# Moving four loads of a linear-attention and feed-forward kernel to later places in the load queue

## The chip, the cores and the metric

The kernel runs on one core of one Trainium2 chip. The metric is the device time of one execution in microseconds (us); lower is better. The core has a matrix engine (TensorE, PE in the profile), a vector engine (VectorE, DVE), a scalar engine (ScalarE, ACT), GpSimd (POOL) and SyncE (SP), which here only issues transfers. Each engine works through its own instructions in order and waits on semaphores for the others. Transfers (DMAs) run beside the engines, on 16 DMA engines that the queues share.

## The reference

The first block is a linear attention with a decaying state (4 batches, 8 heads, 768 tokens, 48 channels a head), the second a feed-forward layer on its output (3072 tokens, 384 channels, 2048 hidden):

```python
for t in range(S):
    cur = np.einsum('bhd,bhe->bhde', u[None] * kt, vt)
    y[:, :, t] = np.einsum('bhd,bhde->bhe', rt, state + cur)
    state = wt[:, :, :, None] * state + np.einsum('bhd,bhe->bhde', kt, vt)
...
h = x @ w_in
sp = np.maximum(h, 0.0) + np.log1p(np.exp(-np.abs(h)))
g = h * erf(sp)
return (g @ w_out)
```

All data is float32 outside, except that the weights arrive as 64-bit floats: the kernel loads them as pairs of 32-bit words.

## The kernel before, in words

**Steps.** The tokens are cut into 12 steps: 6 stretches of 128 tokens by 2 pairs of batches. Step s needs r and k (`in`, 1024 KB, loaded in two halves), w (512 KB) and v (384 KB). The inputs' buffers `in`, `w` and `v` exist twice, so step s + 2 uses the buffers of step s.

**Attention in levels.** Within halves of 64 tokens, the decayed scores are built in six levels. Level l multiplies the right halves of blocks of 2^l tokens with the left ones on TensorE (`level_products`, L552). VectorE then puts the scores into `own` (`take_level`, L562, or L569 on ScalarE for level 6; L773 and L908 for level 1) and scales r and k in place by products of w (`scale`, L321 in step 0, L328 later). Those products of w, `tot_sb`, are made on GpSimd (L350 in steps 0 and 1, L402 from step 2 on). After the levels come the products of scores and v (`from_own`, L584), k turned by TensorE (L817 or L929), the products of the state (`state_part`, L658), which read k and v, and those of r with the state (`through_state`, L610). Step 0 is written out in `attend_first`, steps 1 to 4 in `attend`, the later ones in `attend_late`. In step 0 the second half of the state's products and the sum `S_next` (L852) are held back as `pending` and done in step 1 after level 2's scaling.

**Weights.** There are 16 pairs of weight rows, 0 to 7 of `w_in` and 8 to 15 of `w_out`. Each pair goes through `convert`: stage "l" loads it as two DMAs of 384 KB into a `words` buffer (three of them); "b" (L255, later L257) and "r" (L263) on ScalarE make two parts; "h" (L272) on VectorE shifts one; "o" (L285) on GpSimd adds them. "j" is "h" and "o" together. A load can be held back: `load(i, behind)` first copies one element of another tile into the buffer, on GpSimd (L240) or ScalarE (L238), and the DMA must wait for that copy. `send("brl")` runs the next pair of each named stage.

**Order.** The program order inside each engine is written out by hand (`manual_schedule`), SP's too, so a DMA on SP that waits holds up all that follow on SP. In step 1, each level calls `early` (stage "j" of one pair, before the level is taken) and then `place` (stages "b", "r", mostly "l" of later pairs, then a piece of the feed-forward layer of step 0: L1018, twelve matmuls of `hidden`, and the copy L1027 on ScalarE). The first pieces of `hidden` need xT of step 0: `through_state` copies y (L618), `hop` mixes it (L625) and copies xT (L631); `hop` also issues the loads of pair 3, behind xT, and pair 4. The tile `m` in PSUM exists twice, so a piece waits for the copy L1027 of the piece two before it.

**The loads around the change, in SP's order before:** pair 1 (level 2 of step 0), v[0], w[1], w[2], v[1], pair 2 (behind `own` after level 6), pair 3 and pair 4 (in `hop`), v[2] (`load_third`, after `pending`), pair 5 (`place` of level 2 of step 1), the two halves of in[2], pair 6 (level 3), pair 7 (level 4), pair 8 (level 5), pair 9 and w[3] (level 6).

Of the kernel before, what the change touches and what calls it, by code (L numbers as in the profile page):

```python
# [20 lines left out]
HC = 64  # L21
# [40 lines left out]
def kernel(  # L62
# [14 lines left out]
    nc = tc.nc  # L77
# [99 lines left out]
        nc.scalar.copy(t[:, 0, 0, 0:1], behind)  # L177
        load_halves(t, rkw[1])

    def load_third():  # L180
        t = ins.tile([P, 2, JP, C], FP32, name="in")
        vt = ins.tile([P, NH, D], FP32, name="v")
        loaded[2] = t, vt
        load_v(2)

    def load_v(s):

        vt = loaded[s][1]
        nc.sync.dma_start(out=vt[:], in_=v[s])
# [113 lines left out]
    def rows(e, n=D):  # L303
        return slice(e * EP, e * EP + n)
# [440 lines left out]
    def attend_first(xT):  # L745


        for _ in prepare(0):
            pass
        totals = plan_totals(0)  # L750
        c, _, vt, made, S, S_next, ends = parts_of(0)
        t5 = turns["first"]
        own = att.tile([P, NH, HC], FP32, name="own")
        halves = [range(j * NP, (j + 1) * NP) for j in range(NJ)]
        batch = JP * C // 2 // NJ
        pp = products([P, NE, JP, HC])
        for half in halves:
            level_products(pp, by_pair(made), 1, half)
            stay_warm(2)
        nc.scalar.copy(first[:], mask_sb[:, 0, :])  # L760
        totals(1, part=slice(0, batch))
        for j in range(NJ):
            scale(0, 1, batch=j)
        load_second(t5[:, 1, 0, NP - 1, 1:2])

        def wait_for(t):

            nc.gpsimd.tensor_copy(out=block_sb[:, 0:1], in_=t5[:, 1, 0, NP - 1, t : t + 1])

        wait_for(1)  # L770
        totals(1, part=slice(batch, 2 * batch))
        totals(2, part=slice(0, batch // 2))
        nc.vector.tensor_mul(  # L773
            own[:], pp[:].rearrange("p e n t -> p (e n) t"),
            first[:, None, :].to_broadcast([P, NH, HC]),
        )
        behind = {3: (3,), 4: (4, 5), 5: (6,)}
        for level in range(2, LOG):
            pp = turns.pop("pp", None) or products([P, NE, JP, HC])
            for j, half in enumerate(halves):  # L780
                level_products(pp, first_pair, level, half)
                scale(0, level, batch=j)
            turns["pp"] = products([P, NE, JP, HC])
            keep_busy(turns["pp"], (DM,))
            take_level(own, pp, level)
            wait_for(1 << level - 1)
            if level == 2:
                totals(2, part=slice(batch // 2, batch))
            else:
                totals(*behind[level])  # L790
            if level == 2:
                stages["b"](0, 0)
                stages["b"](0, 1)
                stages["r"](0)
                for _ in prepare(1):
                    pass
                stages["l"](1, own[:, 0, 2:3])
                nc.sync.dma_start(out=vt[:], in_=v[0])
                nc.sync.dma_start(out=ws[1][:], in_=rkw[1][:, 2])
                load_w(2)  # L800
                load_v(1)
        totals = plan_totals(1)
        pp = turns.pop("pp")
        for j, half in enumerate(halves):
            level_products(pp, first_pair, LOG, half)
            scale(0, LOG, batch=j)
        take_level(own, pp, LOG)

        kT = att.tile([P, NH, D], FP32, name="kT", bufs=1)
        kT_by_e = kT[:].rearrange("p (e n) d -> p e n d", e=NE)  # L810
        turned = [products([P, NE, JP, HC])]
        keep_busy(turned[0], (DM,))
        for j, half in enumerate(halves):
            if j:
                turned.append(products([P, NE, JP, HC]))
            for i, n in enumerate(half):
                nc.tensor.transpose(  # L817
                    turned[j][:, 0, 2 * i : 2 * i + 2], first_pair(1, n), ident[:]
                )
        from_own(0, own, 1)  # L820
        for half, ps, copy in zip(halves, turned, (nc.scalar.copy, nc.vector.tensor_copy)):
            copy(
                kT_by_e[:, :, half.start : half.stop],
                ps[:, 0].rearrange("p (n e) d -> p e n d", e=NE)[..., :D],
            )
        stages["l"](2, own[:, 0, HC // 2 : HC // 2 + 1])
        stages["b"](1, 0)
        stages["b"](1, 1)
        fence()
        stages["h"](0)  # L830
        stages["h"](0)
        ps = [[products([P, NE, JP, HC], 1 - e)[:, e] for e in range(NE)]]
        state_part(0, kT, ps, (0,))
        from_own(0, own, 0)
        nc.scalar.copy(middle[rows(1)], ps[0][1][rows(1), :, :D])
        nc.vector.tensor_copy(middle[rows(0)], ps[0][0][rows(0), :, :D])
        stages["r"](1)
        stages["h"](1)
        stages["h"](1)
        wait_for(HC - 1)  # L840
        stages["o"](0)
        nc.gpsimd.tensor_mul(faded[1][:], middle[:], ends[:, :, 1:2].to_broadcast([P, JP, D]))
        totals(1)
        stages["o"](1)
        totals(*range(2, LOG + 1))
        through_state(0, xT)

        def pending():
            part = products([P, NE, JP, HC], turns["next"])[:, 0]
            state_part(0, kT, ps + [[part] * NE], (1,))  # L850
            for e in range(NE):
                nc.vector.tensor_add(S_next[rows(e)], faded[1][rows(e)], part[rows(e), :, :D])  # L852

        turns["pending"] = pending

# [18 lines left out]
    def attend(s, xT, early, place, behind):  # L874
# [11 lines left out]
        for level in range(near_log(s) + 1 if s == DIRECT else 1, LOG + 1):  # L886
            rk = by_pair(made) if level == 1 else RK
            pp = turns.pop("pp", None) or products([P, NE, JP, HC])
            if s == level == 1:
                level_products(pp, rk, level, range(NP))  # L890
                turns.pop("hop")()
                level_products(pp, rk, level, range(NP, JP))
                send("br")
            elif s != 2 or level != 2:
                level_products(pp, rk, level)
            if level == LOG and s == DIRECT:
                spread_blocks(s + 1, pp)
            if s == 1 and level == LOG:
                early(level - 1)
            scale(s, level)  # L900
            if s == 1 and level == 2:
                turns.pop("pending")()
                load_third()
            if s != 1 or level < LOG:
                early(level - 1)
            got = pp[:].rearrange("p e n t -> p (e n) t")
            if level == 1:
                nc.vector.tensor_mul(  # L908
                    own[:], got, first[:, None, :].to_broadcast([P, NH, HC])
                )  # L910
            else:
                take_level(own, pp, level)
            if level > 1:
                next(following, None)
            if s == 2 and level == 1:

                def ahead():
                    turns["pp"] = products([P, NE, JP, HC])
                    level_products(turns["pp"], RK, 2)

                turns["ahead"] = ahead
            place(level - 1)
            if s == 1 and level == 2:
                load_halves(loaded[2][0], rkw[2])

        from_own(s, own, 1)
        ps = products([P, JP, P])
# [346 lines left out]
    with tc.manual_schedule(  # L1274
# [15 lines left out]
        for s in range(n_steps):  # L1290
# [7 lines left out]
            def place(n):  # L1298
# [7 lines left out]
                if s in ALONE:  # L1306
                    if s == 2 and not n:

                        next(hids[0])
                        turns.pop("ahead")()  # L1310
                    convert_at(n)
                    if (s, n) == (1, LOG - 1):
                        load_w(3)
                    if (s, n) == (2, LOG - 2):
                        load_v(3)
                        nc.sync.dma_start(out=block_sb[:], in_=block_mask)
                        nc.sync.dma_start(out=u_row[:], in_=u_rows)
                    if s == 2 and not n:
                        beside(s, next(places))
                        advance(STAGES[s][n])  # L1320
                        return
                    advance(STAGES[s][n])
                else:
                    advance(STAGES[s][n])
                    convert_at(n)
                    if s == DIRECT - 1 and not n:
                        load_rows(DIRECT)
# [125 lines left out]
```

## Time and profile before

| What | us |
|---|---|
| median of 6 runs (588.48 to 590.86) | 589.61 |
| the profiled execution: its time | 590.34 |
| its span, first to last instruction | 588.5 |
| TensorE busy | 579.7 (98%) |
| VectorE busy | 438.6 (75%) |
| ScalarE busy | 361.1 (61%) |
| GpSimd busy | 271.3 (46%) |

The granted TensorE clock is full throughout. "Busy" of TensorE counts matmuls that are pipelined and whose ends are modelled, so 98% does not mean peak rate. In lists of instructions a line gives the start in us, the length in us, engine, line of the kernel, operation, output <- inputs, how many are merged, and in brackets how long the engine had been idle before and what ended that. In the chain of work that ended last, a line gives start, length and what ran; "issue" is time in which the engine waited for nothing that the profile shows. In a table of stretches a line gives the stretch, its length, the busy time of each engine with its number of instructions, the granted clock, the busy share of the DMA engines, and GB/s.

### The profile page before, as it was taken

How to read it: one execution, taken by the hardware profiler on the slowest of the kernel's cores; microseconds unless marked ns; L12 is line 12 of the kernel's file. 1: busy time of each engine (PE TensorE's matmuls, PEld its weight loads, DVE VectorE, ACT ScalarE, POOL GpSimd, SP SyncE). 2: the span in 40 equal slices, each digit the busy share in tenths (PEclk: the TensorE clock that was granted, in tenths of full speed). 3: DMA queues.
4: the chain of work that ended last, by engine and by line, in shares of the span. 5: the costliest groups of instructions: out<-in, count | busy, mean ns of one | idle time of the engine just before them, and what ended most of it. 6: DMA issues, size and time to landing. Idle time of an engine off the chain costs nothing.

```text
span 588.5 us, 16632 instructions
## 1 busy us (share of the span) xinstructions
PE 579.7 (98%) x7256; PEld 498.2 (85%) x7256; DVE 438.6 (75%) x523; ACT 361.1 (61%) x474; POOL 271.3 (46%) x307
## 2 busy tenths in 40 slices
PE   8899999999999999999999999999999999999997
PEld 6688887688668668998998998998998898898997
DVE  6686886999996899799799799799799525023140
ACT  3658877644444698756766766766766754746720
POOL 3556381703398379469369369369369000000000
PEclk9999999999999999999999999999999999999999
DMA  7695662340342414244334334333331300000000
GB/s 242 237 320 195 217 218 70 154 154 12 142 144 74 133 43 166 42 142 153 57 136 158 57 133 153 65 128 114 74 125 37 74 21 14 3 20 15 1 27 28
DMA packets 54081, 63.24 MB, mean 107 GB/s; under 512 B 35160, under 2 KB 40568, under 8 KB 52984
## 3 DMA queue, kind: packets, MB, share of 16 engines
q1 hardware_dynamic: 53624, 61.98, 33.1%
q8 instruction: 57, 0.93, 0.6%
q10 hardware_dynamic: 384, 0.20, 0.1%
q14 instruction: 16, 0.13, 0.1%
HBM read 52.39 MB, written 8.69 MB: 104 GB/s over the span
## 4 chain that ended last, share of the span: by engine, by line
PE 84%; DVE 9%; ACT 2%; issue 2%; DMA 2%; POOL 0%; SPq 0%; DVEq 0%; POOLq 0%; ACTq 0%
PE m L1018 36%; PE m L1126 28%; PE m L1050 6%; PE pp L552 4%; DVE in L328 2%; PE y L584 2%; PE pp L658 2%; PE y L610 2%; PE m L860 1%; DVE sums L453 1%; DMA words<-in_moe_w_in 1%; DVE words L467 1%; DMA rest<-in_w_rows 1%; DVE rk L463 1%; ACT rest L263 1%
## 5 line engine op out<-in xcount | busy, mean ns | idle before, releaser
L1018 PE MATMUL m<-xT,w_in_sb 128*128 128x256 f32 x1152 | 256.7, 381 | 0.5 <-ACT h L1027 0.4
L1018 PEld LDWEIGHTS m<-xT,w_in_sb 128*128 128x128 f32 x1152 | 216.2, 190 | 31.0 <-ACT h L1027 0.8
L1027 ACT COPY h<-m 128x512 f32<-128x512 f32 x96 | 55.6, 580 | 81.8 <-PE m L1018 81.8
L328 DVE TENSOR_TENSOR in<-in,tot_sb 128x1024 f32<-128x1024 f32 (+1 forms) x55 | 79.3, 1443 | 15.0 <-PE pp L552 13.1
L463 POOL TENSOR_TENSOR rk<-words 128x528 f32<-128x528 f32 (+3 forms) x28 | 42.4, 1514 | 91.1 <-DVE sums L453 80.7
L467 POOL TENSOR_TENSOR words<-words,rest 128x528 f32<-128x528 f32 (+10 forms) x77 | 78.2, 1016 | 6.0
L1050 PE MATMUL m<-w_out_sb,h 128*128 128x384 f32 x192 | 64.3, 491 | 0.0
L1050 PEld LDWEIGHTS m<-w_out_sb,h 128*128 128x128 f32 x192 | 35.7, 190 | 23.5
L1126 PE MATMUL m<-mixed,h 128*128 128x192 f32 x288 | 51.1, 331 | 0.0
L974 ACT ACT_TABLE_LOAD x36 | 46.2, 1283 | 2.5 <-issue 1.9
L1126 PE MATMUL m<-w_out_sb,h 128*128 128x192 f32 x272 | 47.5, 329 | 0.0
L1126 PEld LDWEIGHTS m<-mixed,h 128*128 128x128 f32 x288 | 46.6, 190 | 0.9
L978 ACT ACT_TABLE_LOAD x36 | 46.2, 1283 | 1.6 <-DVE room L1109 1.1
L1126 PEld LDWEIGHTS m<-w_out_sb,h 128*128 128x128 f32 x272 | 44.3, 190 | 0.4
L1126 PE MATMUL m<-w_out_sb,room 128*128 128x192 f32 x256 | 44.2, 326 | 0.0
L552 PEld LDWEIGHTS pp<-in 48*64 48x64 f32 (+1 forms) x2368 | 33.4, 126 | 12.1 <-issue 4.0
L1126 PEld LDWEIGHTS m<-w_out_sb,room 128*128 128x128 f32 x256 | 42.0, 190 | 0.0
L983 DVE TENSOR_TENSOR h<-h,y 128x1024 f32<-128x1024 f32 x17 | 20.7, 1216 | 28.3 <-ACT y L978 28.1
L974 ACT ACTIVATE room<-h 128x1024 f32<-128x1024 f32 x36 | 38.1, 1059 | 0.4
L552 PE MATMUL pp<-in 48*64 48x32 f32 (+1 forms) x2368 | 37.1, 212 | 0.6 <-DVE in L328 0.5
L983 DVE TENSOR_TENSOR h<-h,pp 128x1024 f32<-128x1024 f32 x19 | 23.1, 1214 | 19.1 <-ACT pp L978 19.1
L463 POOL TENSOR_TENSOR words<-words 128x336 f32<-128x336 f32 (+6 forms) x49 | 35.2, 718 | 3.8
(144 smaller groups left out, 824.6 us busy)
## 6 DMA issues: line engine op xcount, KB each, us to landing
in<-in_rkw SPq DMA_DIRECT2D x8, 1024.0 KB, 5.0
words<-in_moe_w_in SPq DMA_DIRECT2D x16, 384.0 KB, 5.4
words<-in_moe_w_out SPq DMA_DIRECT2D x16, 384.0 KB, 4.7
words<-in_rk_rows SPq DMA_DIRECT2D x8, 768.0 KB, 5.6
w<-in_rkw SPq DMA_DIRECT2D x11, 512.0 KB, 5.4
v<-in_v SPq DMA_DIRECT2D x12, 384.0 KB, 5.9
out<-o SPq DMA_DIRECT2D x23, 192.0 KB, 2.8
in<-in_rkw SPq DMA_DIRECT2D x7, 512.0 KB, 5.8
```

The source lines that it names most:

```text
L328: nc.vector.tensor_mul(halves, halves, view(tots[level - 1], 0, [[1, n], [2, nb], [0, half]]))
L463: engine.tensor_mul(terms[n], r[:, :, n:], k[:, :, : near - n])
L467: engine.tensor_mul(k[:, :, :m], k[:, :, :m], w[:, :, n : n + m])
L552: nc.tensor.matmul(to, lhsT=rk(1, n)[rows(e), s0 : s0 + m], rhs=right, start=True, stop=True,)
L584: nc.tensor.matmul(y[at(e, p), e, p // 2, j, t], lhsT=vt[t, n * NE + e, :], rhs=own[t, e * JP + n, :], start=swap == 1 and not j and not q ...
L974: nc.scalar.activation(sp_room, chunks[0], AF.Softplus)
L978: nc.scalar.activation(at, sp_room, AF.Erf)
L983: nc.vector.tensor_mul(h, h, at)
L1018: nc.tensor.matmul(ps[:, ff, :], lhsT=w_in_sb[:, g * FG + f + ff, kk * P : (kk + 1) * P], rhs=xT[:, kk, :], start=kk == 0, stop=kk == KT - 1,)
L1027: nc.scalar.copy(h[:, f : f + FT, :], ps[:])
L1050: nc.tensor.matmul(ps[j][:], lhsT=gs[g][:, f, j * C : (j + 1) * C], rhs=w_out_sb[:, g * FG + f, :], start=g + f == 0, stop=g == NG - 1 and ...
L1126: nc.tensor.matmul(to, lhsT=a[:, f], rhs=b[:, f], start=start and f == 0, stop=f == FG - 1, skip_group_check=True,)
```

## The change

Four loads move. In step 0, after level 2, w[2] and v[1] are no longer issued. Pair 2 ("l" of 2) moves from before the fence to after stage "o" of pair 0, behind `middle` (the state after the first half) in place of `own`. `load_third` moves into `pending`, after `S_next`; it now loads v[1] behind an element of `S_next`, by a copy on GpSimd, and no longer v[2]. w[2] is issued after in[2], in level 2 of step 1. v[2] is issued after w[3], in the `place` of level 6 of step 1. Nothing else is added or removed.

```diff
-    def load_third():
+    def load_third(behind):
+
         t = ins.tile([P, 2, JP, C], FP32, name="in")
         vt = ins.tile([P, NH, D], FP32, name="v")
         loaded[2] = t, vt
-        load_v(2)
+        nc.gpsimd.tensor_copy(out=loaded[1][1][:, 0, 0:1], in_=behind)
+        load_v(1)
...
                 nc.sync.dma_start(out=ws[1][:], in_=rkw[1][:, 2])
-                load_w(2)
-                load_v(1)
...
-        stages["l"](2, own[:, 0, HC // 2 : HC // 2 + 1])
         stages["b"](1, 0)
...
         stages["o"](0)
+        stages["l"](2, middle[:, 0, 0:1])
         nc.gpsimd.tensor_mul(faded[1][:], middle[:], ends[:, :, 1:2].to_broadcast([P, JP, D]))
...
                 nc.vector.tensor_add(S_next[rows(e)], faded[1][rows(e)], part[rows(e), :, :D])
+            load_third(S_next[:, 0, 0:1])
...
                 turns.pop("pending")()
-                load_third()
...
                 load_halves(loaded[2][0], rkw[2])
+                load_w(2)
...
                         load_w(3)
+                        load_v(2)
```

## The prediction

> **What bounds the kernel now.** I read the page's header and chain first. TensorE is busy 98% of the span and 84% of the chain that ended last is TensorE, so an edit in the first 50 us counts only by how far it shifts the step that starts TensorE's unbroken run. Then I read the chain in order of time for 20 to 60 us:
>
> ```profile
> 22.06 0.65 PE pp L658 x20
> 22.71 1.58 issue
> 24.30 0.43 PE pp L658 x10
> ...
> 24.81 0.47 ACT middle L835
> ...
> 28.29 0.93 ACT xT L631 x3
> ...
> 29.83 5.46 DMA words<-in_moe_w_in
> ```
>
> Two things stand out: TensorE stops for 1.58 us in the middle of step 0's state products, waiting for nothing that the profile shows, and ScalarE then waits for weight pair 3, whose load is issued behind xT. The stretches, with the DMA engines' busy share and GB/s last, say why:
>
> ```profile
> 16.00:21.00 5.00, 4.76 (x141) 3.15 (x141) 4.53 (x8) 3.60 (x9) 1.85 (x7) 1.00 1.00 377
> 21.00:25.00 4.00, 2.33 (x98) 1.86 (x97) 1.90 (x5) 1.51 (x4) 1.78 (x1) 1.00 0.93 347
> 25.00:30.00 5.00, 4.66 (x124) 3.77 (x114) 2.40 (x4) 3.27 (x8) 4.55 (x4) 1.00 0.06 19
> ...
> 33.00:37.00 4.00, 4.00 (x89) 3.36 (x86) 3.68 (x4) 1.60 (x2) 0.88 (x1) 1.00 1.00 340
> 37.00:42.00 5.00, 4.60 (x102) 3.87 (x95) 4.97 (x6) 3.27 (x6) 2.50 (x2) 1.00 0.99 386
> 42.00:47.00 5.00, 5.00 (x83) 4.22 (x82) 5.00 (x4) 4.39 (x10) 2.91 (x2) 1.00 1.03 400
> ```
>
> DMA is full from 16 to 25, idle from 25 to 30 and full again from 33 to 47. In the first full stretch the trace's packet records have one 16 KB packet on the instruction queue, at 21.86 (0.91 us long). TensorE's 768th instruction record lies at 18.77; after the 256th (10.99), 512th (15.21) and 1024th (24.79) the next such packet starts 0.0 to 0.6 us later, here 3.1 us. So I take the 1.58 us for a fetch of instructions held up behind data; TensorE goes on 1.5 us after that packet's end.
>
> Last, the timeline of ScalarE (L255 converts pair after pair) and VectorE:
>
> ```profile
> 29.34 0.87 ACT L255 ACTIVATE y<-words 128x768 f32<-128x768 f32 x1
> ...
> 35.40 0.87 ACT L255 ACTIVATE y<-words 128x768 f32<-128x768 f32 x1 [4.34 <-DMA words<-in_moe_w_in]
> ...
> 41.40 0.88 ACT L255 ACTIVATE y<-words 128x768 f32<-128x768 f32 x1 [1.73 <-DMA words<-in_moe_w_in]
> ...
> 45.98 0.89 ACT L255 ACTIVATE y<-words 128x768 f32<-128x768 f32 x1 [0.60 <-DMA words<-in_moe_w_in]
> ...
> 49.07 0.94 ACT L255 ACTIVATE y<-words 128x768 f32<-128x768 f32 x1 [0.90 <-DVE w_in_sb L272]
> ```
>
> These are pairs 2, 3, 5, 6 and 7. Three wait for their words. VectorE runs from 30.24 to 49.04 with idle times of 0.52 and 0.31 us only. So from 30 to 50 the limits are DMA and VectorE, with TensorE close behind (idle 0.7 us).
>
> **The change, part by part.** Sizes: a pair is 2 x 384 KB = 0.79 MB, a v 0.39, a w 0.52, in[2] 1.05.
>
> 1. *The stretch freed.* From 15.7 to 25.2 DMA moves pair 1, v[0], w[1], w[2], v[1] and pair 2: 3.4 MB. Without the last three 1.70 MB are left, at 377 GB/s done by 20.2. The fetch then starts by 20.3 and is of use by 20.3 + 0.9 + 1.5 = 22.7, just where TensorE ran dry. Gain on TensorE between 0 (fetch as late as now) and 1.58; I take 1.5. What is late next is ScalarE: its two L255 on pair 1 end at 23.69, then L835 (0.47), L263 (0.94), L618 (0.37), the hop's L625 (1.58) and L631 (0.93) run in a row: xT at 28.1 in place of 29.2. Gain 1.1, not 1.5.
>
> 2. *Pair 2 behind `middle`.* The copy on GpSimd (0.18 us in the row of 20.67) now stands behind stage "o" of pair 0 (L285, ends 25.03). So SP issues pair 2 at about 25.3 and 25.65, not 20.88. What covers it: DMA idle from 25 to 30. Bounds for its landing: 3.8 us from the second issue (pair 0, issued 8.13, its second L255 at 12.03) and 5.4 (the page's median for these loads). On idle engines pair 0 is nearer: 29.5. L255 on pair 2 starts at 29.5, not 29.34: **+0.15**, and all that ScalarE had won is lost at this wait. Queued behind it on ScalarE are L263 and pair 3's L255; on VectorE, L272 of pair 2 (30.24), then L908 and the level scalings. The other end, 5.4, makes it 31.1. The copy also delays L842 by 0.2 us; the step-1 totals behind it have over 2 us in hand.
>
> 3. *VectorE from 30.4.* L272 0.96, L908 1.22; the 0.52 idle before the scaling of level 2 goes, because TensorE is 1.1 earlier with the products that this scaling overwrites; L328 2.11, L852 1.11: S_next at 35.5, not 36.0. Pair 3, issued 1.1 earlier, is there, so the 0.31 before its L272 goes too: **-0.8** on VectorE from here.
>
> 4. *v[1] behind S_next takes v[2]'s place.* SP is in order. Now:
>
> ```profile
> 33.50 0.33 SPq L189 DMA_DIRECT2D v<-in_v  x1
> 34.01 0.81 SPq L147 DMA_DIRECT2D words<-in_moe_w_in  x2
> 34.86 0.92 SPq L147 DMA_DIRECT2D in<-in_rkw  x2
> ```
>
> v[2] waited for L658 (33.46). v[1] waits for S_next (35.5) and a GpSimd copy (0.2; GpSimd is idle 3.52 us there): issued at 35.8. Behind it on SP stand pair 5 (36.3, 2.3 us later than now), in[2] and w[2]. Meanwhile pairs 3 and 4 are over by about 33.5, so DMA idles some 3 us. v[1] itself is not needed before L584 at 51.79.
>
> 5. *w[2] behind in[2].* Before pair 6 lands there must move, from about 36.8 (1 us after the first issue): v[1], pair 5, in[2], w[2] and pair 6: 3.54 MB. At 386 to 400 GB/s that takes 9.0 us, to 45.8; add 1.5, as pair 2 now lands at 26.7 though DMA is full only to 25.2: 47.3. Bounds: 46.0 (at 426 GB/s, among the best slices of the first full stretch, and 0.9 us to landing) and 48.2 (pair 7 shares as it does now: 0.76 MB more moved before pair 6 landed, at 378 GB/s). Pair 6 landed at 45.9, so its L255 starts 1.3 later, at 47.3. Pair 5 lands near 41.8 by the same count; its L272 is due at 43.4, so it costs nothing.
>
> 6. *Behind pair 6 on ScalarE:* L263 and L1027 now end at 48.17 and pair 7's L255 waits 0.90 for VectorE. So 0.9 of the 1.3 fits, and L255 of pair 7 starts at 49.5: **+0.4**. It decides, through L263, L1027 and L569 (51.17, now 51.6), when step 1's L584 on TensorE (52.39) starts. VectorE's 0.8 is lost here. From that L584 the chain is TensorE nearly without a break to 69 us, and then conversions that are issued from it; I carry the shift 1:1 to the end.
>
> 7. *v[2] behind w[3].* Issued at about 49.5 onto engines idle from 53 on (share 0.02 between 53 and 60); its first reader is L584 at 84.40. No cost: 30 us in hand. w[2]'s first reader is L402 on GpSimd (47.04); it may come 0.5 us late and is off the chain. Per-issue times on SP (0.43) lie in SP's waits.
>
> **Sum:** step 1's L584 moves by +0.15 (pair 2), -0.95 (VectorE's two waits and shorter wait behind), then +1.2 (pair 6 in place of VectorE as the last): +0.4. The profiled execution took 590.34 us, its span 588.5; it would become 590.7. The median of the runs shown is 589.61, 0.73 less, so there I predict **590.0**. A measurement of this kernel can tell about 0.2%, 1.2 us, from no change.
>
> [...]
>
> **Rivals.**
> - *The front gain survives:* pair 6 lands by 46.4, as the best slices allow; then VectorE decides, -0.8: 588.8. If pair 2 also lands in 3.2 us (pair 0's first half: issued 7.76, converted at 10.97), VectorE starts 0.6 sooner: -1.4, 588.2. For: the 0.9 of slack before pair 7. Against: 3 us of idle DMA.
> - *SP's queue held by v[1] makes it slower:* pair 2 lands after 5.4 us, S_next comes at 37.0, so pair 5 is issued at 37.8 and pair 6 lands near 48.8 to 49: L255 of pair 6 2.9 late less 0.9: +2.0, 591.6. It decides once pair 6 lands after 48.1 (0.9 slack plus 1.2). For: pair 3 now takes 5.46 on nearly idle engines. Against: pair 4 is issued right behind pair 3, nothing behind pair 2.
> - *The change doesn't do what it says:* the stop stays. Then `middle` is at 25.3, pair 2 is issued at 25.6, and all of points 4 to 6 come 0.7 later: +1.1, 590.7.
>
> **Chances.** Forecast 0.47, front gain 0.16, SP held 0.22, stop stays 0.15. Faster by over 0.2%: 0.11 (most of the first rival's lower half). Slower by over 0.2%: the second rival, half of the third, and a sixth of the forecast: 0.36. Within: 0.53. Range: 588.5 to 591.6, from the first rival to the second, with the bounds of point 5 (46.0 and 48.2, -0.8 and +1.3) inside.
>
> **What would show it.** Right: no stop of over 0.3 us inside L658 near 22.7; xT's copies end near 28.1; pair 2's L255 at 29.5 marked as waiting for DMA; DMA share low around 34 to 36; v[1] issued near 35.8; pair 6's L255 near 47.3 waiting for DMA; step 1's L584 within 0.5 us of 52.4. Wrong: a stop of TensorE elsewhere by another fetch; DMA over 420 GB/s from 37 on; pair 7's L255 waiting for VectorE still, which would mean a gain; a shift at 52 us that does not reach the end.

## The result, and the profile after

| | before | changed |
|---|---|---|
| median, us | 590.26 (47 runs) | 594.54 (21 runs) |
| profiled execution, us (span) | 590.34 (588.5) | 594.39 (592.6) |
| mean granted TensorE clock, profiled execution | 1.0 | 0.994 |

The ratio is 1.0071, 95% interval 1.0059 to 1.0082: 4.2 us slower, well outside the range given (588.5 to 591.6). Two executions below were slow throughout, the profiled one of e2_pair2_only (667.8 us at a granted clock of 0.85) and one of g4_pair2_scalar_unheld (993.1 us at 0.557), and are left out of the ratios, not of the medians.

The chain of the changed kernel, in order of time. Most lines of code are 1 to 2 higher than before: L257 is L255, L265 L263, L274 L272, L330 L328, L554 L552, L586 L584, L660 L658, L1019 L1018, L1028 L1027; L842, L852 and L908 keep their numbers. In the runs below lines lie a few numbers off (L906 in f2 is L908).

```profile
24.96 1.20 POOL words L242
...
26.55 5.10 DMA words<-in_moe_w_in
...
31.67 0.85 ACT y L257
...
33.42 1.23 DVE own L908
...
34.69 1.52 PE pp L660 x32
36.21 5.17 PE m L1019 x12
41.38 1.06 PE pp L554 x64
```

The stop of 1.58 us inside the state's products is gone. In its place the chain runs through GpSimd's one-element copy, pair 2's load, pair 2's L257, VectorE's L908 and the pending state product. The twelve matmuls behind that take 5.17 us; before, such a group took 2.8. TensorE's timeline before, then that of the changed kernel with its stretches (granted clock third from the end), say why:

```profile
31.59 1.14 PE L552 MATMUL pp<-in 48*64 48x32 f32 x64
32.55 0.91 PE L658 MATMUL pp<-v,kT 64*48 64x48 f32 x32
33.39 2.86 PE L1018 MATMUL m<-xT,w_in_sb 128*128 128x256 f32 x12
36.18 1.14 PE L552 MATMUL pp<-in 48*64 48x32 f32 x64
```

```profile
22.03 0.88 PE L660 MATMUL pp<-v,kT 64*48 64x48 f32 x30
...
30.42 1.14 PE L554 MATMUL pp<-in 48*64 48x32 f32 x64
34.69 1.52 PE L660 MATMUL pp<-v,kT 64*48 64x48 f32 x32 [3.13 <-DVE own L908]
36.14 5.24 PE L1019 MATMUL m<-xT,w_in_sb 128*128 128x256 f32 x12
```

```profile
31.60:34.70 3.10, 0.01 (x2) 0.01 (x2) 2.15 (x3) 2.58 (x4) 1.19 (x2) 0.92 0.86 325
34.70:36.20 1.50, 1.50 (x33) 1.41 (x33) 1.50 (x1) 1.24 (x2) 0.77 (x1) 0.50 0.08 25
36.20:38.00 1.80, 1.80 (x6) 1.45 (x5) 1.75 (x4) 0.00 (x0) 0.19 (x1) 0.50 0.00 0
38.00:41.30 3.30, 3.30 (x9) 2.36 (x7) 1.93 (x2) 1.70 (x2) 1.83 (x1) 0.54 0.69 224
41.30:45.00 3.70, 3.70 (x77) 3.22 (x76) 2.43 (x3) 0.89 (x2) 0.19 (x1) 1.00 0.87 319
```

TensorE is 1.2 us ahead of before at 30.42, then idles 3.13 us, and the clock is halved from 34.18 to 41.0 (6.83 us, by the trace's clock record). The next level's products start at 41.31, not 36.18: 5.1 us late. Of that, 2.1 is the late start of the pending product (34.69 for 32.55) and 3.0 the half clock (0.6 on L660, 2.4 on L1019). Slack later gives 1.2 back: step 1's L586 is through at 57.0, not 53.0, and the span is 4.1 longer. ScalarE's conversions of pairs 2, 3 and 6:

```profile
31.67 0.85 ACT L257 ACTIVATE y<-words 128x768 f32<-128x768 f32 x1 [3.40 <-DMA words<-in_moe_w_in]
...
33.78 0.87 ACT L257 ACTIVATE y<-words 128x768 f32<-128x768 f32 x1 [0.45 <-DMA words<-in_moe_w_in]
...
50.58 0.91 ACT L257 ACTIVATE y<-words 128x768 f32<-128x768 f32 x1 [1.92 <-DMA words<-in_moe_w_in]
```

Pair 2 is 2.3 us later than before, pair 3 is 1.6 sooner, pair 6 4.6 later.

### The profile page after: what moved, and what is told of

Its sections match the earlier page's. It is cut to its first block, busy times and chain, and to the rows that moved or that the text cites. A ratio compares the mean times of both kernels' runs of the same rounds, so it can differ in the third digit from the quotient of the medians.

```text
span 592.6 us, 16635 instructions
## 1 busy us (share of the span) xinstructions
PE 582.7 (98%) x7256; PEld 500.3 (84%) x7256; DVE 435.7 (74%) x523; ACT 361.2 (61%) x474; POOL 271.6 (46%) x308
## 4 chain that ended last, share of the span: by engine, by line
PE 85%; DVE 10%; issue 2%; ACT 1%; DMA 1%; POOL 0%; SPq 0%; DVEq 0%; POOLq 0%
PE m L1019 38%; PE m L1127 28%; PE m L1051 6%; PE pp L554 5%; DVE in L330 2%; PE y L586 2%; PE pp L660 2%; PE y L612 2%; PE m L861 1%; DVE words L469 1%; DVE rk L465 1%; DVE sums L455 1%; DMA words<-in_moe_w_in 1%; PE pp L870 1%; DVE h L1008 1%
## 5 line engine op out<-in xcount | busy, mean ns | idle before, releaser
L1019 PE MATMUL m<-xT,w_in_sb 128*128 128x256 f32 x1152 | 259.2, 384 | 0.1
L1019 PEld LDWEIGHTS m<-xT,w_in_sb 128*128 128x128 f32 x1152 | 217.8, 191 | 31.7 <-ACT h L1028 0.6
L1028 ACT COPY h<-m 128x512 f32<-128x512 f32 x96 | 55.5, 580 | 83.4 <-PE m L1019 83.3
L330 DVE TENSOR_TENSOR in<-in,tot_sb 128x1024 f32<-128x1024 f32 (+1 forms) x55 | 75.5, 1372 | 20.0 <-PE pp L554 13.9
L1127 PE MATMUL m<-w_out_sb,h 128*128 128x192 f32 x272 | 47.5, 329 | 0.0
L554 PEld LDWEIGHTS pp<-in 48*64 48x64 f32 (+1 forms) x2368 | 33.4, 126 | 11.9 <-issue 5.0
L404 POOL TENSOR_TENSOR tot_sb<-tot_sb 128x256 f32<-128x256 f32 (+4 forms) x50 | 36.2, 724 | 3.8
L554 PE MATMUL pp<-in 48*64 48x32 f32 (+1 forms) x2368 | 37.3, 212 | 0.4 <-DVE in L330 0.2
```

Of the source, the lines that this page charges most:

```text
L330: nc.vector.tensor_mul(halves, halves, view(tots[level - 1], 0, [[1, n], [2, nb], [0, half]]))
L404: nc.gpsimd.tensor_mul(new, pair[:, :, 0], pair[:, :, 1])
L554: nc.tensor.matmul(to, lhsT=rk(1, n)[rows(e), s0 : s0 + m], rhs=right, start=True, stop=True,)
L1019: nc.tensor.matmul(ps[:, ff, :], lhsT=w_in_sb[:, g * FG + f + ff, kk * P : (kk + 1) * P], rhs=xT[:, kk, :], start=kk == 0, stop=kk == KT - 1,)
L1028: nc.scalar.copy(h[:, f : f + FT, :], ps[:])
L1127: nc.tensor.matmul(to, lhsT=a[:, f], rhs=b[:, f], start=start and f == 0, stop=f == FG - 1, skip_group_check=True,)
```

## Experiments

The theory, **PS**: two causes, taken to hide one another. P is the late pair 2, which stops TensorE before the pending product. S is the SP queue held by v[1], which makes pair 6 late and stops TensorE before its sixth piece. In either stop the clock may be halved, which adds to it. The rivals were that S alone is the cause, and that the places of w[2] or v[2] are.

Medians are us; ratios are to the kernel before, timed in the same series of runs, with 95% intervals. There were four series (e, f, g, h), in which the kernel before had medians of 591.68, 590.52, 590.68 and 591.22, so a difference of 0.1 or 0.2% between ratios of two series says little.

### e1_pair2_back

The changed kernel with pair 2 in its old place.

```diff
+        stages["l"](2, own[:, 0, HC // 2 : HC // 2 + 1])
         stages["b"](1, 0)
...
-        stages["l"](2, middle[:, 0, 0:1])
```

> The changed kernel with pair 2's load back in its old place (behind own, before the fence); v[1], w[2] and v[2] stay late. Theory P (late pair 2): pair 2's L257 on ScalarE starts at about 28.3 us in place of 31.7, TensorE does not stop before the pending state product (3.1 us in the changed kernel), no half clock near 34 to 41; time 1 us under the kernel before to equal with it, that is ratio 0.998 to 1.000 (about 589.5 where before is 590.3). Theory S (the SP queue held by v[1], so pairs 5 and 6 late): these loads are as late as in the changed kernel, so most of the 4.2 us stays; ratio over 1.004. Theory R (prediction's sum without the late pair 2): pair 6 still eats the gain; ratio 1.000 to 1.001.

Measured: 594.12, ratio 1.0037 (1.0015 to 1.0060). P alone is refuted as the whole cause. The wait for L908 is gone, and half of the loss is still there. TensorE and ScalarE in this kernel:

```profile
47.80 0.76 PE L554 MATMUL pp<-in 48*32 48x32 f32 x64
52.29 5.20 PE L1019 MATMUL m<-xT,w_in_sb 128*128 128x256 f32 x12 [3.74 <-ACT h L1028]
```

```profile
42.32 0.90 ACT L257 ACTIVATE y<-words 128x768 f32<-128x768 f32 x1 [3.23 <-DMA words<-in_moe_w_in]
...
50.03 0.84 ACT L257 ACTIVATE y<-words 128x768 f32<-128x768 f32 x1 [3.73 <-DMA words<-in_moe_w_in]
50.81 0.87 ACT L265 ACTIVATE rest<-words 128x768 int32<-128x768 uint32 x1
51.59 0.56 ACT L1028 COPY h<-m 128x512 f32<-128x512 f32 x1
```

v[1] is issued at 36.13 and pair 6 lands near 50. On ScalarE the copy L1028 of the fourth piece stands behind pair 6's L257 and L265; the sixth piece needs the buffer m which that copy frees. So TensorE idles 3.74 us, and again runs at half clock (from 50.3, 6.83 us). In the changed kernel the same late pair 6 (50.58) stopped nobody, because TensorE was already late by more.

### e4_pair2_seen

As e1, but pair 2 behind the fence's output (`seen`, VectorE's small copy from y), ahead of stage "o".

```diff
         fence()
+        stages["l"](2, seen[:, 0:1])
...
-        stages["l"](2, middle[:, 0, 0:1])
```

> The changed kernel with pair 2's load behind the fence's output (seen, ready near 22.1 us) and ahead of stage o of pair 0 on GpSimd, so issued at about 22.4 us. Theory P: pair 2 lands before xT is ready, its L257 starts at about 28.3 us; as without the move: ratio 0.998 to 1.000. Theory S: ratio over 1.004. If being issued later than 20.9 us is in itself harmful, it stands between e1_pair2_back and the changed kernel.

Measured: 594.07, ratio 1.0042 (1.0018 to 1.0066). As e1: issuing pair 2 as late as this is not harmful in itself, and the loss of e1 is still there. Its profiled execution held the full clock and took 590.73, though TensorE stopped 2.58 us before the sixth piece:

```profile
50.35 2.83 PE L1019 MATMUL m<-xT,w_in_sb 128*128 128x256 f32 x12 [2.58 <-ACT h L1028]
```

### e2_pair2_only

The kernel before with pair 2 alone moved behind middle.

> The kernel before with only pair 2's load moved behind middle. Theory P: the stop of TensorE inside the state products stays (w[2] and v[1] are early), pair 2 is issued at 25.5 to 26 and lands at 30 to 31; its L255 is 1 to 1.7 us late, TensorE waits about 1.2 us for L908 before the pending product, which is too short to halve the clock; time +1 to +1.7 us, ratio 1.002 to 1.003. Theory S: nothing on SP is held longer, ratio 0.999 to 1.001.

Measured: 590.93, ratio 1.0003 (0.9974 to 1.0031). Rather a miss for P, which had 1.002 to 1.003 here: alone, without the front gain, the move costs at most about 1.8 us (the upper end of the interval), perhaps nothing. That 1.2 us of idling is too short to halve the clock is not shown: behind a stop of 1.58 us the profile of the kernel before stayed at 1.0, behind one of 1.18 us f4's (below) went to half.

### e3_warm, g1_warm6, g2_unheld_warm6

Matmuls of the identity in the stop before the pending product: 14, then 6, then 6 together with an SP queue that is not held.

```diff
             if s == 1 and level == 2:
+                warm = ps_m.tile([P, NC, P], FP32, name="m")
+                for _ in range(6):
+                    nc.tensor.matmul(
+                        warm[:], lhsT=ident[:],
+                        rhs=ident[:, None, :].to_broadcast([P, NC, P]),
+                        start=True, stop=True,
+                    )
                 turns.pop("pending")()
```

> The changed kernel with 14 matmuls of the identity into a free buffer m between level 2's products and the pending product of step 1, so that TensorE is busy while pair 2 is awaited (3 us of added work in the 3.1 us stop). Theory P with the clock as the second half of the loss: no half clock from 34 to 41; the twelve matmuls after the pending product take 2.9 us and not 5.2. If the clock alone is left over, the time falls by 2 to 3 us under the changed kernel (ratio to before 1.002 to 1.004). If pair 6, landing at 50.5 us, is right behind as the next limit, only 0.6 to 0.8 us come back (ratio 1.0055 to 1.0065). Theory S without the clock: no change, ratio 1.007.

> The changed kernel with 6 matmuls of the identity (2.7 us) in the 3.1 us stop before the pending product; e3_warm had 6.3 us of them, twice what fits. Theory PS: the clock stays full from 30 to 42, the pending product and the twelve matmuls behind it take 0.9 and 2.9 us (1.5 and 5.2 in the changed kernel), 3 us; but then TensorE waits for pair 6, which lands near 50, before its sixth piece (stop of 2 to 3 us), so little comes back: ratio to before 1.004 to 1.007. If the halved clock alone were what the late pair 2 costs: 1.001 to 1.003.

> f2_pair2_late_unheld (pair 2 late, v[1] not held) with the same 6 matmuls. Theory PS: neither the halved clock nor pair 6 is left, only the late start of the pending product, 2.1 us late against before, some of which later slack takes: ratio 1.001 to 1.003, granted clock 1.0 in most runs. If the clock has no part: as f2_pair2_late_unheld, 1.004.

Measured: e3 598.46, ratio 1.0122 (1.0094 to 1.0151); g1 594.91, 1.0065 (1.0040 to 1.0091); g2 592.65, 1.0036 (1.0012 to 1.0060). e3 was badly sized: its matmuls took 6.31 us, twice what fits. It still shows that with TensorE kept busy there the clock stayed full: all its four runs had 1.0, and the twelve matmuls took 2.86, not 5.24. In g1 the extra tile took a buffer of m, so the next piece waited 1.71 for a copy, and the clock was halved there for 3.41 us; it does not tell the two shares apart. In g2 eight of twelve runs held a clock of at least 0.999, median 591.8. Against 589.6 for the kernel before at that clock (table below) this is 2.2 us of waiting without the clock. That is near the 2.1 read above, though later slack took a part of that one. The whole ratio lies just above what was expected and no better than f2's 1.0040 below, which was the expectation for a clock without a part. So what the clock costs is read from the trace and from the sorted runs (g2 at full clock 591.8, f2 592.5 and 594.1); no ratio shows it.

### f1_back_unheld

Pair 2 in its old place (the diff of e1), and SP not held: w[2] and v[1] behind pair 6.

```diff
-        nc.gpsimd.tensor_copy(out=loaded[1][1][:, 0, 0:1], in_=behind)
-        load_v(1)
...
                 load_halves(loaded[2][0], rkw[2])
-                load_w(2)
+            if s == 1 and level == 3:
+                load_w(2)
+                load_v(1)
```

> Pair 2's load back in its old place, and v[1] no longer held behind S_next: w[2] and v[1] are issued behind pair 6, in level 3 of step 1; v[2] late as in the changed kernel. Theory PS (two independent causes, late pair 2 and the SP queue held by v[1], each enough to stop TensorE for 2.5 to 3.7 us, with the clock halved on top in most runs): both are gone, pair 5 is issued by 31 us, pair 6 lands before 43, TensorE has no stop over 1 us from 20 to 56, and what is left is the front gain: 0.8 to 1.5 us under the kernel before, ratio 0.9975 to 0.9990. If something else in the moved loads costs (w[2] or v[2] in the later stretches), ratio over 1.001.

Measured: 589.94, ratio 0.9983 (0.9968 to 0.9998). Both causes taken away, the loss is gone. v[2] is still late here, so its place costs nothing that shows. ScalarE's pair 6 does not wait (pair 7, behind w[2] and v[1], does):

```profile
44.34 0.91 ACT L255 ACTIVATE y<-words 128x768 f32<-128x768 f32 x1
48.50 0.88 ACT L255 ACTIVATE y<-words 128x768 f32<-128x768 f32 x1 [1.94 <-DMA words<-in_moe_w_in]
```

### f2_pair2_late_unheld

The changed kernel with SP not held (the diff shown under f1); pair 2 stays behind middle.

> The changed kernel with only the hold of v[1] undone (w[2] and v[1] behind pair 6, level 3); pair 2 stays late behind middle. Theory PS: pair 2's L257 waits until about 31.7 us, TensorE stops about 3 us before the pending product and then runs at half clock; pair 6 is in time. As pair 6 was hidden behind this in the changed kernel, little comes back: ratio 1.004 to 1.007. If the held queue alone had been the cause: ratio 0.998 to 1.000.

Measured: 593.47, ratio 1.0040 (1.0020 to 1.0059). P stands without S:

```profile
35.51 1.52 PE L658 MATMUL pp<-v,kT 64*48 64x48 f32 x32 [3.66 <-DVE own L906]
36.96 5.18 PE L1019 MATMUL m<-xT,w_in_sb 128*128 128x256 f32 x12
```

This is the lower edge of what was expected, so undoing S gave back more than PS said (0.3 of 0.7%). Each cause alone costs 0.4% (e1, f2), both together 0.7%, neither nothing (f1). By these times the two nearly add up; that one hides the other is seen in the traces only, one execution each: the late pair 6 stops TensorE in e1 and not in the changed kernel. And P costs 0.4% only along with the front gain: without it, e2's interval ends at 0.3%.

### f3_v1_held_only, f4_w2_only

Of the change only v[1] behind S_next (and v[2] late); only w[2] behind in[2].

> Of the change only v[1] behind S_next in v[2]'s place, and v[2] late; w[2] early and pair 2 in its old place as before. Theory PS: pair 5 is issued near 36.5, pair 6 lands 1.3 us (w[2]'s 0.52 MB) sooner than in e1_pair2_back, at 47.5 to 48.6; TensorE stops 1.5 to 2.5 us before step 1's sixth piece; ratio 1.001 to 1.003. If w[2] behind in[2] is what makes pair 6 late, ratio 0.998 to 1.000.

> Of the change only w[2] behind in[2]; v[1], v[2] and pair 2 as before. Theory PS: SP is not held, pair 6 lands about 1.3 us later than before (47.3), 0.9 of which fits; against it a part of the front gain: ratio 0.999 to 1.001. If w[2]'s place is the cause of e1_pair2_back's loss: ratio 1.003 or more.

Measured: f3 591.96, ratio 1.0014 (0.9997 to 1.0032); f4 590.96, 1.0003 (0.9984 to 1.0022). Both near what was expected; neither interval excludes 1. In f3's trace pair 6's L257 starts at 47.61 and TensorE stops 1.68 us. f4's trace has a stop of 1.62 too, with pair 6 at 50.54; that execution was late from the front on, with half the clock from 25.0. The two together (e1) cost more than the sum of the two medians. So S stands for both, v[1]'s hold and w[2] ahead of pair 6, which f1 and f2 undo together; what each of them costs alone is not shown.

### g4_pair2_scalar_unheld

f2, with pair 2's copy behind middle made by ScalarE right after it makes its half of middle.

```diff
+        stages["l"](2, middle[:, 0, 0:1], True)
         stages["r"](1)
...
-        stages["l"](2, middle[:, 0, 0:1])
```

> f2_pair2_late_unheld with pair 2's copy behind middle made by ScalarE ahead of L263 of pair 1, and not by GpSimd behind stage o: issued at about 24.4 us. Theory PS: the place behind middle is not what costs, but the 1.2 us copy on GpSimd and pair 3 close behind: pair 2 lands by 28.5, its L255 starts within 0.5 us of xT, no stop before the pending product; ratio 0.997 to 0.9995. If any load of pair 2 behind middle is too late: ratio over 1.002.

Measured: 590.46, ratio 0.9991 (0.9970 to 1.0011). The same place in the data, but pair 2 issued 1 us sooner (25.1) and 3 us and more ahead of pair 3: its L255 waits 0.15 us only.

```profile
24.93 0.19 ACT L238 COPY words<-middle 128x1 f32<-128x1 f32 x1
...
29.30 0.88 ACT L255 ACTIVATE y<-words 128x768 f32<-128x768 f32 x1 [0.15 <-DMA words<-in_moe_w_in]
```

### g3_pair3_early, h1_v1_behind_7, h2_seen_v1_behind_7

Attempts at a version better than both: f1 with v[1] behind pair 7; in g3 also pair 3 behind middle; in h2 also pair 2 behind seen.

```diff
             if s == 1 and level == 3:
                 load_w(2)
+            if s == 1 and level == 4:
                 load_v(1)
```

> A version meant to be faster: f1_back_unheld with pair 3's load moved from behind xT to behind middle (copy on ScalarE, issued near 24.3 us, onto idle DMA engines), and v[1] behind pair 7 in level 4. Theory PS: pair 3's L255 starts at 29 to 30 and not 33.8, no ScalarE wait for DMA over 1 us until 50; VectorE is the limit: 0.5 to 1.5 us under f1_back_unheld, ratio to before 0.996 to 0.998. If DMA in that stretch holds up the fetch of instructions again: a stop of TensorE between 24 and 32 and ratio over 0.999.

> f1_back_unheld with v[1] behind pair 7 (level 4) and w[2] behind pair 6. Theory PS with the front stop as the trigger of the halved clock in the kernel before: pair 7's wait of 1.9 us at 48.5 goes, step 1's L584 starts 0.3 to 0.6 us sooner; granted clock 1.0 in most runs against about a third of the runs of before; ratio 0.997 to 0.9985. If f1's gain was an accident of its runs: ratio 0.9995 to 1.001 and as many runs under full clock as before.

> As h1_v1_behind_7, but pair 2's load behind the fence's output (seen), issued near 22.4 us onto idle DMA engines, so that the stretch of the state's products is free of all three loads. Theory PS: as h1_v1_behind_7 or 0.2 to 0.5 us less; ratio 0.9965 to 0.9985, no stop of TensorE over 0.3 us in L658. If pair 2 beside the next instruction fetch costs more than it saves: a new stop between 24 and 30, ratio over 0.999.

Measured: g3 591.43, ratio 1.0002 (0.9985 to 1.0019); h1 589.27, 0.9973 (0.9959 to 0.9987); h2 589.76, 0.9977 (0.9962 to 0.9992). g3 missed: pair 3 came 3 us sooner, but TensorE shows stops marked "issue" of 1.4, 0.8 and 0.5 us between 18 and 60, with the DMA engines at a share of 0.87 to 0.99 during them; each time TensorE goes on 1.2 to 1.5 us after the end of a packet on the instruction queue, as in the kernel before (1.5). h1 and h2 are faster than both kernels, h1 by 0.27%. Where their gain comes from is seen when runs are sorted by their mean granted clock (number of runs, median us):

| kernel | 0.999 and over | 0.996 to 0.997 | 0.994 and less |
|---|---|---|---|
| before (112 runs of four series) | 34: 589.6 | 35: 590.5 | 43: 592.2 |
| changed (22, one more than above) | none | 4: 594.2 | 18: 594.5 |
| e1_pair2_back | 1: 591.8 | 7: 594.1 | 2: 595.0 |
| f2_pair2_late_unheld | none | 5: 592.5 | 7: 594.1 |
| f1_back_unheld | 10: 589.8 | 2: 590.7 | none |
| h1_v1_behind_7 | 10: 589.1 | none | 2: 591.2 |
| h2_seen_v1_behind_7 | 11: 589.7 | none | 1: 591.4 |

6.83 us of half clock in the changed kernel's profile go with a mean of 0.994, 3.41 us in g1's with 0.997. The mean is 0.997 or less in 78 of 112 runs of the kernel before, in 3 of 24 of h1 and h2, in 2 of 12 of f1. At full clock h1 is 0.5 us faster than before, f1 and h2 no faster, so most of their gain is that the clock is kept, and at most 0.5 of the 1 us and more won at xT is in their time. In the profile of before, which happened to hold the full clock, this part of the worth of removing its stop could not be seen. At equal clock e1 is no faster than the changed kernel, as far as so few runs tell: what bringing pair 2 back in time alone wins there shows as fewer runs with 0.994 or less (2 of 10, and 18 of 22).

A halving right behind a stop at the front is seen in two profiles only, f4's (half clock from 24.98) and h1's (from 23.15; there the stop lies just before the state's products):

```profile
24.31 0.43 PE L658 MATMUL pp<-v,kT 64*48 64x48 f32 x11 [1.18 <-issue]
```

```profile
22.83 0.86 PE L584 MATMUL y<-own,v 64*48 64x64 f32 x32 [1.91 <-DMA v<-in_v]
```

That the front stop does this in the runs of the kernel before is inferred: the profiles of f1 and h2, both at full clock, have stops there of only 0.5 and 0.2 us, and most runs of these kernels keep the clock (10 and 11 of 12).

## Why the prediction was wrong, point by point

In short: the sum's +0.15 for pair 2 became +2.3, the path from pair 2 to TensorE was not in it, and a halved clock had no term. The -0.95 for VectorE turned into a loss with pair 2, and pair 6, 4.6 us late and not 1.3, was not what TensorE waited for in this profile.

1. *The stretch freed: right in this profile.* The instruction packet starts at 20.25 (20.3 forecast), 1.5 us behind TensorE's 768th instruction record at 18.75 and not 3.1 as before; the stop goes, and xT's copies end at 28.04 (28.1). That the late packet makes the stop fits the profiles: with it 1.5 us behind TensorE does not stop, with 2.0 (f1) 0.5 us, with 2.3 (g3) 0.8, with 2.8 (f4) 1.2, with 3.1 (before) 1.6, with 3.7 (h1, where the profile names v[0]) 1.9. But the gain is not sure: f2, g1, g2 and e3 have the same front as the changed kernel, and there the packet starts 1.75 to 2.4 us behind and TensorE stops for 0 to 0.8 us.

2. *Pair 2 at 29.5: wrong by 2.2 us, the first step that failed.* Two sizes were off. The copy on GpSimd took 1.19 us, not 0.18:

```profile
23.20 1.83 POOL L287 TENSOR_TENSOR w_in_sb<-w_in_sb,rest 128x768 int32<-128x768 int32 x1 [2.37 <-ACT m L257]
24.96 1.19 POOL L242 COPY words<-middle 128x1 f32<-128x1 f32 x1
```

```profile
24.36 1.75 DVE L330 TENSOR_TENSOR in<-in,w 128x1024 f32<-128x1024 f32 x1
```

These are GpSimd and VectorE of the changed kernel. The copy ends 0.04 us after L330, and likewise 0.05 after it in f2 (26.44 and 26.39) and g2 (26.12 and 26.07). The front gain itself had moved L330 (26.16 before) onto the copy. So the copy took longer beside L330; what couples the two is not shown, nor do the starts show which came first (in g2 the copy's record starts at 24.51, L328's at 24.86). And the load took 5.1 us from its second issue, not 3.8: pair 3, also 1.1 us earlier by the front gain, is issued 2.1 us behind pair 2's first half. (In g4, with pair 3 3.7 us behind its second half, pair 2 took 3.8.) The other bound (5.4) was nearer, and the forecast chose against it because "nothing" stood behind pair 2.

3. *VectorE 0.8 us ahead: wrong, an edge was missed.* The pending product writes the PSUM buffer that L908 reads, and L908 stands behind pair 2's shift on VectorE. So pair 2 holds TensorE too. S_next came at 37.6, not 35.5:

```profile
36.48 1.11 DVE L852 TENSOR_TENSOR s<-faded,pp 48x384 f32<-48x384 f32 x2
```

4. *v[1] at 35.8: right as a mechanism, 2 us later through step 3* (37.86 in the changed kernel; 35.35 to 36.13 in e1, e4 and f3, where pair 2 was in time).

5. *Pair 6 at 47.3: too early.* With v[1] on time it landed at 48.0 (e4) to 49.9 (e1), near or over the upper bound of 48.2; without w[2] ahead of it (f3), at 47.5.

6. *What stands behind pair 6: the wrong waiter.* Pair 7's L257 was priced, with 0.9 us of slack. The copy L1028 behind pair 6 also frees a buffer m for TensorE's sixth piece, which was not in the list: 2.6 to 3.7 us of stop (e4, e1), not 0.4.

7. *v[2] and w[2]: no cost.* For v[2] right as far as the runs show (f1 keeps it late). For w[2] none is seen alone (f4, 1.0003), but ahead of pair 6 it adds to S: e1, with it, is at 1.0037, and f3, without it, at 1.0014.

Left out altogether was the clock: the forecast took 1.0 from the one profile and had no term for a stop that halves it. It is 3.0 us of the 5.1 above. In the trace it is halved (0.50 in the stretches above) for 6.83 us with 3.13 us of idling; in g1 3.41 us of half clock came with a stop of 1.71 us, and in f4 a half clock that takes its mean to 0.994 with one of 1.18.

Of the rivals, "SP's queue held by v[1]" was right that a late S_next holds pair 5 and pair 6 (pair 5 issued at 38.37 in the changed kernel, 37.8 by the rival; pair 6 landed at 50.5, not 49). e1 has about its price (2.2 us over before; 2.0 forecast), but that is luck: in e1 pair 2 is in time, the wait goes through L1028 to TensorE, and half clock is in it. In the profile of the changed kernel the late pair 6 stops nobody, and TensorE is late through pair 2.

## What to carry to other kernels

When a load is moved behind a new trigger, follow all that waits for it to every engine, through buffers that its consumers must free as well: here one pair of weights held TensorE for 3.13 us through a PSUM buffer that a waiting VectorE instruction still had to read. SP issues its loads in order here (v[1] at 37.86 and pair 5 behind it at 38.37, against 34.01 before), so put no wait for a late result into such a queue ahead of loads that are due sooner; the same loads placed behind them cost nothing that shows (ratio 0.9983 in f1, 0.9973 in h1). And when a loss is half explained, undo each part and both: the trace of the changed kernel shows no wait of TensorE for pair 6, and yet e1 lost 0.4% with that wait alone.

## What was not expected of the hardware

- In the changed kernel the stop of TensorE cost about twice itself: 3.13 us of idling came with 6.83 us at half clock, 3.0 us more. A stop of 2.58 us (e4's profile) left the clock at 1.0, so it is not certain in a single run; in the kernel before, 78 of 112 runs have a mean clock of 0.997 or less.
- The length of a stop alone does not settle it. The profiles show the clock halved in or right after stops of 1.18 us (f4), 1.71 (g1), 1.91 (h1), 3.13 (changed kernel), 3.66 (f2) and 3.74 (e1), and still full after stops of 1.58 (before), 1.62 (f4's second), 1.68 (f3) and 2.58 (e4). What else decides is not shown.
- A one-element copy on GpSimd took 1.19 us beside a VectorE operation with two inputs (changed kernel), and 0.18 us with VectorE idle (before, at 20.67).
- A 16 KB instruction packet started 3.1 us after TensorE's 768th instruction record with the DMA engines full (share 1.00 from 16 to 21 us, before), 1.5 to 2.4 us in the eight profiles without w[2], v[1] and pair 2 ahead of it, and TensorE stood for 1.58 us in the first case.
